# Gates of an mLSTM as one pass over half-sequence rows, with a new order of the first 560 steps

## The chip, the cores and the metric

The kernel runs on one core of one Trainium2 chip. The metric is the device time of one execution in microseconds (us). The engines are TensorE (PE; PEld are its weight loads), VectorE (DVE), ScalarE (ACT), GpSimd (POOL) and SyncE (SP), which here only issues DMAs. Each engine works off its own queue in order.

## The reference, cut

An mLSTM attention over 4 batches, 8 heads, 768 tokens and heads of 40 is followed by a feed-forward block (320 to 2048 to 320) and a mixture of 8 experts of which each token takes one. The part that matters here:

```python
for t in range(S):
    m_new = np.maximum(f_gate[:, :, t] + m, i_gate[:, :, t])
    f_stab = np.exp(f_gate[:, :, t] + m - m_new)
    i_stab = np.exp(i_gate[:, :, t] - m_new)
    m = m_new
    C = f_stab * C + i_stab * outer(v_t, k_t)
    n = f_stab * n + i_stab * k_t
    h = C @ q_t
    y[:, :, t] = sigmoid(o_gate) * h / max(|n @ q_t|, 1)
h = x @ w_in                                   # x: y laid out as 3072 tokens x 320
x = (max(h, 0) + alpha * min(h, 0)) @ w_out
# then, with e the argmax of x @ w_gate:
# out = softmax weight * sigmoid(x @ w_output_gate)[e] * (relu(x @ w1[e]) @ w2[e])
```

## The kernel before

**Tiling.** The attention runs in 24 units: 4 batches (b) times 6 chunks (c) of 128 tokens, all 8 heads at once. Three units make a block of 384 tokens, and the feed-forward block takes 8 such blocks times 16 slices of 128 hidden columns, 128 products `ph` (code F, line 916) and 128 accumulations `acc` (code S, lines 950 to 953). The expert weights stream through the core meanwhile (el, es, et: load, split in two float parts, store). After about 537 us comes the expert phase, which the change leaves alone. Weights of the feed-forward block arrive as 64-bit words: each of 16 slices of `w_in` (li) and `w_out` (lo) is loaded into one of three buffers `raw`, decoded by three DVE instructions (di, do; lines 655, 657, 659) and split in a high and a low part by ACT and by DVE or POOL (si, so). From each slice of `w_out`, PE also makes three transposes (gw, `pw`), ACT copies them (gc), and PE multiplies them with the routers' weights (gv, `pwg`, six instructions).

**A unit of attention.** `kt` are keys times a gate (pt), `pd` their products with the values (ad), `state` the running state (au: mask, then decay and add). `D` is a matrix of decays, loaded from the DRAM tensor `gd` with a broadcast (load_g) and raised to exponentials on ACT (ae, line 749). `ps` are scores (as), multiplied with D (am) and applied to the values, `pa` (ab). `pb` is the history (ah), normalised into `hN` (an) and added (aa); ay has the steps that divide and gate the result, and ac and ax transpose it into the feed-forward block's input.

**The gates before.** `gi` and `gf` hold 32 rows (batch and head), three times over, by 768 tokens. Three parts cover 1, 2 and 3 chunks. In each, one scan gives the running maximum `m` (line 549), differences follow, and scans by chunk give the cumulative sum `G` (line 566), stored in `gd`. `w` holds three sets of 32 rows: exp(G), exp of the key weights, and an exponent offset. PE transposes it by chunk (`pe_ek`, line 595) into `EKT`, which pt, an and ae read; `pe_dec` (line 613) spreads the decay of each chunk over 120 rows into `DEC`, which au reads. The parts are tied by the last maximum, `mlast`.

**What sets the order.** Every engine's order is the order in which the program names the work. For the first phase that is the list `ORDER`: codes of steps, each next use of a code being the next item of its kind. Sets in `OTHER` choose the second of two engines for single items of a kind. Buffers are few: three PSUM banks for attention, two for `ph`, three tiles `xr` and two `v`, which the gates share with the transposed weights and with the activations, and two `so`, which the gates' input shares with the output gates. A load waits in SP's queue, with all behind it, until its buffer is free.

Of the kernel before, what the change touches and what calls it, by code (L numbers as in the profile page):

```python
# [17 lines left out]
P = 128  # L18
# [6 lines left out]
E = 8  # L25
# [26 lines left out]
        0, 1, 3, 4, 5, 6, 7, 9, 15, 17, 20, 22,  # L52
    ),
    "prep_kt": (
        0, 1, 2, 3, 4, 7, 8, 9, 13, 14, 15, 16,
    ),
    "att_y": (
        3, 4, 6, 7, 11, 13, 16, 17, 18, 19, 20, 21, 22, 23,
    ),
    "expert_split": (  # L60
        0, 2, 3, 5, 6, 7, 8, 10, 12, 13, 14, 15, 18, 19, 20, 25, 26, 27, 30, 31, 32, 33, 34, 35, 36, 37,
        38, 39, 40, 41, 42, 43, 44, 45, 46, 47, 48, 49, 50, 51, 52, 53, 54, 55, 56, 57, 58, 59, 60, 61,
        62, 63,
    ),
    "gates_w": (
        0, 2,
    ),
    "split_wi": (
        1, 5, 6, 7, 8, 9, 11, 13, 14,
    ),  # L70
    "split_wo": (
        1, 3, 5, 6, 8, 9, 11, 13, 14, 15,
# [5 lines left out]
for _n, _w in (  # L78
    ("ident", P), ("stri", P), ("ones", P), ("bmask", 123),
    ("iota32", 32), ("iota128", P), ("tokv", U), ("rev", E), ("rst", E * (U - 3)),  # L80
    ("indb", B), ("nmin", E), ("nadd", E),
):
    CONST_COLS[_n] = (_o, _w)
    _o += _w
CW = _o

# [6 lines left out]
ah si li li so ad di di di ae lq lo aa gc ay si ay gv load_g load_gates ay di an sg lo di si ay au ah do gs di ae  # L93
lq an as do di load_g load_g lv do gw lo am gates di so do do ac ax lq lq si ab gc lo lo ae do ae aa ay ay ay as ay
gw lo am ab lv do do lg so ac gates_g gates_st gv do gates_w gc aa ay ay ay ay li gv log ac so ax do do gs gs li gw
gates_e do do do do gates_d load_g load_g gc ax lo so so gw gc gw gc pt lo F ad pt do do do gw load_g di di so F di
au f gv si di di di ad F do gs f el ah au g S ae do do si lg lg lg an do as gc ae am F f gw do load_g so g do li
load_g gv gv gs f di di li li ah S es F as gc et g S ab lo di lv gs ae so si di di gw ae an li di f F am g S aa di
g load_g gv ay ay di F li di si si log f pt do do F do gw gs lq di gv gc gv ay di di sg ay si di ac g gc gs ad F S
f di di so ab ax f g ae li di li si pt au aa ay ah ae an load_g lv ae g di di f F lo do do lo si lv di do S S di di  # L100
li li lq F S g gw ay ay lg gs gv lq load_g el f ay as so gc g F S S di am di ac di si f f pt do do do F g g load_g
S ax si ad di ab gs di sg aa ad lv au es au f S as so ae di si F am ab ae gw g S ay ay lo gv f ay li di aa di do ay
do gc gv et load_g ay gs ac ah ae di lg ay F g S el gs si load_g load_g as ax load_g f do F el el ay pt F an g S es
am ab es f f g et et so es gw ay ae gc ae g F f F gv gs ah S an aa g f g lq ay ay et el log ay ad au bo el el es es
F f F f lg load_g ae S ac ax load_g lv ae S pt et g S g es ah an lq lv ad au F f ay g F f S as am lq ah an F f et
ab aa ay S g g ac ax el ay et es lv el F f F f as am S g es load_g ae lg lg et ay lq ay S sg S et g F f ab aa ay
load_g bp lg S g ac ax S pt el ad au F f F f S g g S el el es lq es F f g F f g ay ay ay ah an pt S pt S et es F f
S et g F f log ad au g ae et as am ae S bo F f g F f load_g ae ab aa ay el lv el S g ay es el F f as am g load_g
load_g es et es et F f load_g ac ax lv ah an el el ae ae lg lg S g S S F f g ad au pt ah an ay es F f g ab aa F f
ay ad au et ae et S g el load_g el F f es ay et F f ay ay ac ax S g es ae S g ah an F f S S et es ay et g lv el el  # L110
bp as am F f F f el g es et pt S S ab aa ac ax g ad au F f F f g S g ay lq sg es es S ay lv pt F f ay el lq g F f
as am S g F f et es ah an ad au S log S g bo F f sg et g load_g load_g ay el el F f lg S ae ab aa ay ay ay et S F f
S g lq lq S g ae ac ax lg el S as am lv load_g load_g load_g es et es et ay F f pt F f g g ab aa ae ay ac ax F f S
g es ay ay ay S F f F f ae as am lq S g g load_g ah an ad au ac ax ae el F f lv pt el ae g et ab aa ay ay S es es F
f et et g load_g ay F f S g as am ay lv S load_g S F f g F f ah an ab aa ay S el el es ad au lg ay ae g ay el es F
f ac ax g load_g et et ah an ah an lv es et ae bp ay S S S ae as am F f g F f load_g bo g ab aa ae load_g ae F f g
S lq el S ac ax F f g load_g pt S pt F f lg load_g ae as am el es lq F f S g S el g es et F f et g ay ay el F f ae
ab aa g ay ay ay F f load_g lv F f S lq S ad au g g es et es et el ad au pt ae ac ax S F f g S el el as am F f F f
log g S S g es et lg bp es et F f F f g S g S load_g el S es et F f g F f log el el ae ay ay g S S bo es F f lg F f
ah an g S es as am sg ay et et g F f g lq ab aa ay S F f g el el S es load_g load_g sg F f F f S g ay ad au g es ae  # L120
ac ax et S lv et ay ay pt F f es F f ah an ab aa ay ay lg el ae g S g es ay lv ad au pt S F f F f el g ac ax ah an
et es et S load_g ay ae g el el F f es S g lg S ad au F f et es F f lq et et g el el ac ax bp S g S S F f g F f S
es es g F f g et S S bo as am el es F f F f g et lv pt el el et as am ab aa ay es et ay ay load_g S S g lg el
load_g first_set ah an lq ab aa el ay ay F f g F f S g ad au ae es F f F f lv es g S g ac ax S S ae ay ay ay as am
et et es et ac ax F f g F f S el el el bp g F f ah an ab aa g es es ay ay ay ay F f F f S S S g g et es et el S et
el F f g F f el S es es g F f et et ac ax g S S es et F f g ld el el F f g S F f g S bo ld es F f F f S g g route_a
S F f F f S g el g S bh bh bh et ld ld ld ad au bh ld ld bh bh bh F f ld S ld es S ld ld g es F f g bh bh S bh bh F
f g F f S et bh ld g ld S bp F f F f ld bh g bh bh bh bh S S bh route_first bh bh bh g F f route_first2 first_rows
S g F f g ld S F f F f S ld ld g S ld ld ld pt ld ld g first_x first_x S bo bp et first_1 route_b first_1 route_c
first_t first_s first_tl route_c2 first_t first_tl first_s first_2 first_2 route_d first_st first_2 first_2  # L130
"""


STEPS = {
# [72 lines left out]
def mlstm_moe_kernel(  # L207
# [264 lines left out]
    with ExitStack() as p1:  # L472
# [95 lines left out]
        def gates_st(part):  # L568
            c0, c1, o = GPARTS[part]
            nc.sync.dma_start(gd[:, c0 * P : c1 * P], gx[part][0][: B * H])  # L570
# [840 lines left out]
```

## Time and profile before

| | us |
|---|---|
| median of 3 timed runs | 776.0 (774.91 to 776.02) |
| profiled execution | 773.82 |
| its span, first to last instruction | 772.0 |
| PE busy in it | 749.9 |
| DVE, ACT, POOL busy | 472.8, 365.2, 181.4 |

The time around the span is 1.8 us. An instruction's duration is from one profiled execution. PE's instructions overlap in the records: a group's first start to the next group's first start is the pace. Float products of 32 bits are recorded as two instructions each.

### The profile page before, as it was taken

The numbers are of one execution on the slowest core, as the hardware profiler recorded it, in microseconds if no ns is written. First come the engines' busy times: TensorE is split into PE (matmuls) and PEld (weight loads), VectorE is DVE, ScalarE is ACT, GpSimd is POOL, SyncE is SP. The second block draws the span as 40 slices with busy tenths as digits, with TensorE's granted clock in tenths as the row PEclk, the third lists the DMA queues.
The fourth block names the chain that finished last, engine by engine and source line by source line (L and its number), as shares of the span: only waits on it lengthen the run. The fifth ranks groups of instructions, "written<-read, shape, count | busy, mean of one in ns | idle before, by whom it ended". The sixth has DMA issues, their size and how long they took to land.

```text
span 772.0 us, 15194 instructions
## 1 busy us (share of the span) xinstructions
PE 749.9 (97%) x4911; PEld 714.1 (92%) x4911; DVE 472.8 (61%) x1148; ACT 365.2 (47%) x812; POOL 181.4 (24%) x236
## 2 busy tenths in 40 slices
PE   4999999899999999999999999999999999999997
PEld 4889999899999999999999999998999999999996
DVE  6889997757865675777687786867332223223222
ACT  3646766654754555654565354434333333323322
POOL 2444523421231323100000000012222222223223
PEclk9999999999999999999999999999999999999999
DMA  7857869967687967757877968895977744931100
GB/s 227 274 176 199 275 186 292 299 229 242 205 307 253 286 239 222 252 179 273 294 255 267 298 227 292 288 332 201 373 320 269 277 166 170 418 134 36 42 13 22
DMA packets 81787, 179.64 MB, mean 233 GB/s; under 512 B 8700, under 2 KB 39481, under 8 KB 80428
## 3 DMA queue, kind: packets, MB, share of 16 engines
q1 hardware_dynamic: 78252, 169.92, 64.0%
q0 software_dynamic: 3456, 8.71, 3.3%
q8 instruction: 45, 0.74, 0.4%
q14 instruction: 34, 0.28, 0.1%
HBM read 246.55 MB, written 55.59 MB: 391 GB/s over the span
## 4 chain that ended last, share of the span: by engine, by line
PE 80%; DVE 10%; DMA 5%; ACT 3%; issue 2%; POOL 0%; SPq 0%; POOLq 0%; ACTq 0%; DVEq 0%
PE ph L916 19%; PE po L314 13%; PE p L314 13%; PE acc L950 6%; PE acc L951 6%; PE acc L953 6%; PE pa L846 4%; PE p L412 3%; PE ps L759 3%; DMA r_wi<-in_wi_dram 2%; PE pd L811 2%; DMA D<-gd 2%; PE pb L781 1%; PE xt L374 1%; DMA er<-in_ew_dram 1%
## 5 line engine op out<-in xcount | busy, mean ns | idle before, releaser
L916 PE MATMUL ph<-ring 128*128 128x384 f32 x1024 | 198.9, 342 | 0.3 <-DVE ring L938 0.3
L916 PEld LDWEIGHTS ph<-ring 128*128 128x128 f32 x1024 | 178.0, 189 | 2.8 <-DVE ring L938 1.0
L950 PE MATMUL acc<-ring 128*128 128x336 f32 x384 | 123.3, 326 | 0.6 <-ACT ring L937 0.3
L951 PE MATMUL acc<-ring 128*128 128x336 f32 x384 | 119.7, 317 | 0.2 <-DVE ring L716 0.2
L929 ACT ACTIVATE v<-ph 128x384 f32<-128x384 f32 x128 | 62.0, 488 | 103.7 <-PE ph L916 103.5
L434 DVE TENSOR_SCALAR yo<-po,xg 128x320 f32<-128x320 f32 x26 | 14.3, 551 | 137.4 <-PE po L314 137.4
L314 PE MATMUL po<-ring,hh 128*128 (+1 forms) x432 | 95.6, 308 | 0.0
L931 DVE SCALAR_TENSOR_TENSOR ph<-v,al,ph 128x384 f32<-128x384 f32 x104 | 63.9, 619 | 49.2 <-ACT v L929 48.9
L314 PE MATMUL p<-ring,xh 128*128 (+1 forms) x324 | 89.9, 399 | 0.0
L953 PE MATMUL acc<-ring 128*128 128x336 f32 x384 | 80.1, 316 | 0.0
L314 PEld LDWEIGHTS po<-ring,hh 128*128 128x128 f32 x432 | 73.2, 187 | 2.3 <-ACT hh L414 0.2
L938 DVE TENSOR_TENSOR ring<-ph,ring 128x384 fp32r<-128x384 f32 x104 | 57.4, 554 | 29.2 <-ACT ring L937 28.1
L950 PEld LDWEIGHTS acc<-ring 128*128 128x128 f32 x384 | 72.2, 188 | 2.3 <-ACT ring L937 1.0
L951 PEld LDWEIGHTS acc<-ring 128*128 128x128 f32 x384 | 72.2, 188 | 0.5 <-DVE ring L716 0.5
L937 ACT ACTIVATE ring<-ph 128x384 fp32r<-128x384 f32 x104 | 50.6, 488 | 43.6 <-DVE ph L931 36.6
L414 ACT ACTIVATE hh<-p 128x512 fp32r<-128x512 f32 x54 | 29.5, 596 | 86.4 <-PE p L412 86.4
L314 PEld LDWEIGHTS p<-ring,xh 128*128 128x128 f32 x324 | 58.8, 188 | 11.5 <-DMA ring<-scr 0.2
L314 PE MATMUL po<-ring,hl 128*128 (+1 forms) x216 | 66.6, 308 | 0.2 <-DVE hl L416 0.2
L435 POOL DMA_INDIRECT out_dram<-yo,tok x28 | 28.1, 1005 | 161.0 <-DVE yo L434 128.9
L401 ACT ACTIVATE hr<-p 128x512 f32<-128x512 f32 x56 | 33.6, 600 | 67.5 <-PE p L314 62.9
L953 PEld LDWEIGHTS acc<-ring 128*128 128x128 f32 x384 | 63.6, 189 | 0.0
L749 ACT ACTIVATE D<-D,EKT 128x128 f32<-128x128 f32 x192 | 60.7, 393 | 3.9 <-DMA D<-gd 3.7
(201 smaller groups left out, 1189.9 us busy)
## 6 DMA issues: line engine op xcount, KB each, us to landing
ring<-scr SPq DMA_DIRECT2D x26, 3072.0 KB
ring<-scr SPq DMA_DIRECT2D x26, 2560.0 KB
ring<-scr SPq DMA_DIRECT2D x33, 512.0 KB
D<-gd SPq DMA_DIRECT2D x48, 256.0 KB
er<-in_ew_dram SPq DMA_DIRECT2D x32, 384.0 KB
scr<-ring SPq DMA_DIRECT2D x32, 384.0 KB
scr<-er SPq DMA_DIRECT2D x32, 384.0 KB
er<-in_ew_dram SPq DMA_DIRECT2D x32, 320.0 KB
```

What stands on the lines that cost most here:

```text
L314: mm = T.matmul(o_, lhsT, r, start=start, stop=stop)
L401: A.activation(hr_half(j, hf), ph, AF.Relu)
L749: A.activation(d[:, j], d[:, j], AF.Exp, bias=EKT[:, c, i + j : i + j + 1])
L846: T.matmul(pa[:, h * 41 : (h + 1) * 41], t["D", h // 4][:, h % 4], v1[:, h * 41 : (h + 1) * 41], start=True, stop=True,)
L916: T.matmul(ph[:, :384], wi_[i][lo][:, wc], xTs[n % 2][:, xc], start=(a == 0), stop=(a == len(PASSES) - 1),)
L929: A.activation(v, ph[:, :384], AF.Relu, scale=-1.0)
L931: V.scalar_tensor_tensor(g, v, al1[:, i : i + 1], ph[:, :384], ALU.mult, ALU.add)
L937: A.activation(gh, v, AF.Copy)
L938: engine(V, G, "ffn_split", k).tensor_tensor(gl, v, gh.bitcast(F32), ALU.subtract)
L950: T.matmul(ac, gh[:, sl], hi, start=(i == 0), stop=False)
L951: T.matmul(ac, gh[:, sl], lo, start=False, stop=False)
L953: T.matmul(accs[n][t][:, :NO], gl[:, t * P : (t + 1) * P], hi, start=False, stop=(i == NFC - 1))
```

## The change

All six chunks' gates are worked out in one pass. A row is now a batch and head and a remainder k, and holds the chunks k and k + 3 in two groups of 128 columns; 96 rows hold everything once. Within a chunk two scans (a sum and a minimum) need nothing from other chunks. One product with `grep` (gates_b) brings the ends of all chunks to every row, where a scan of six columns gives the maximum at each chunk's start (gates_m). Then come the exponentials (gates_e), three transposes for each half (gates_t, `pe_ek`), and one set of products for all decays (gates_d). The constants are loaded in two pieces, the second late in the order; the selectors become wider and share the `so` buffers. The steps au and ay are cut in two, with the state update in a step av of its own. Single items of an, au and of the row normalisation (att_r) go from DVE to ACT, as 8 or 3 activations each, and the sets in `OTHER` change for the splits, `kt` and y. The list `ORDER` is new for about the first 560 steps; behind that it only has the additional codes av and ay.

```diff
-    "gates_w": (
-        0, 2,
+    "att_n": (
+        3, 5,
+    ),
+    "att_r": (
+        5,
+    ),
+    "att_u": (
+        2, 3, 6,
+    ),
+    "att_v": (
     ),
...
-    ("ident", P), ("stri", P), ("ones", P), ("bmask", 123),
+    ("ident", P), ("bmask", 123), ("stri", P), ("ones", P),
...
+CW0 = CONST_COLS["stri"][0]
...
-lo do lo do do do do load_gates load_cst gw so gc do lo gw gates gates_g load_gates gates_w gates_e load_wg lv do
-do do gw set_al1 gates gates_g gates_w gates_st gv li load_sel lo gc gc lv pt ad au so load_g so gates_st gs
-gates_d lq load_g load_g do gv gs gv gates_e di di gates_d do do pt li as ae gw gs ae di log lg lg ah an am di ab
...
+load_gates load_sel ga ah lo do do do lo do do do gb gm load_cst gw load_wg gc an gw gc so li so di ge gv gv gs gt
+lv lo gates_d do do do gw lq gs di pt so ad au gc gt gates_st lv as di li di load_g load_g pt load_g ae ae di di am
+gv av ab aa si li si lo lg gs di log ae do do do ay ay ay ay lg ad sg ay lq load_g load_g lo au lo lv di load_g lq
+gw di ah av an gc gv gs si ac ax as do do ae am do lo do do ah ab load_g do so so an li ae aa log ay ay ae ay ay lo
+lo gw gw gc gc lq as ay do do do am ac di di di so lo ax do ab aa so si do ay ay gw ay ay do do load_g ay gc gv gs
+set_al1 do load_g do gv gs gv gs pt so ac ax li di di so gw ae ae gc gw gc F F di si f li load_g f gv gs log do do
+do di di g so lg lg gv gs el es g lv ad au F F lq di f lq lo av S lo ae pt as am S lq ah si g do do do do do f ad
...
+        gcon = rp.tile([P, 471], F32, tag="so", name="gcon")[:GR]
+        sel, grep, gkm, gik = gcon[:, :360], gcon[:, 360:456], gcon[:, 456:459], gcon[:, 459:]
...
+        def load_gates():
+            nc.sync.dma_start(ti, gi)
+            nc.sync.dma_start(tf, gf)
+
+        def gates_a():
+            F, u = (hp.tile([P, 384], F32, tag="v", bufs=2, name=nm)[:GR, : 2 * P] for nm in ("gF", "gu"))
+            a, GG = (hp.tile([P, XW], F32, tag="xr", bufs=3, name=nm)[:GR, : 2 * P] for nm in ("ga", "gG"))
+            gx.update(F=F, u=u, a=a, GG=GG)
+            for js in halves:
+                V.tensor_tensor_scan(F[:, js], onesP, tf[:, js], 0.0, ALU.mult, ALU.add)
+            V.tensor_tensor(a, F, ti, ALU.subtract)
+            for js in halves:
+                V.tensor_tensor_scan(u[:, js], onesP, a[:, js], 1e30, ALU.mult, ALU.min)
+            km = gkm.unsqueeze(1).to_broadcast([GR, 2, 3])
+            for q, (x, o) in enumerate(((u, P - 1), (F, P - 1), (a, 0))):
+                xs = x.rearrange("p (j t) -> p j t", j=2)[:, :, o]
+                V.tensor_tensor(st[:, q], xs.unsqueeze(2).to_broadcast([GR, 2, 3]), km, ALU.mult)
+
+        def gates_b():
+            pg = ps_att("pe_g")
+            T.matmul(pg[:GR, :18], grep, small[:, :18], start=True, stop=True)
+            gx["pg"] = pg
+
+        def gates_m():
+            pg, u, a, GG = gx["pg"], gx["u"], gx["a"], gx["GG"]
+            V.tensor_copy(mf, pg[:GR, 6:13])
+            V.tensor_copy(mn[:, 0:1], mf[:, 6:7])
+            V.tensor_tensor_scan(mn[:, 1:6], pg[:GR, 0:5], mf[:, 0:5], 1e30, ALU.min, ALU.subtract)
+            mj = [x.rearrange("p (j k) -> p j k", j=2) for x in (mk, mn)]
+            V.tensor_tensor(mj[0], mj[1], gkm.unsqueeze(1).to_broadcast([GR, 2, 3]), ALU.mult)
+            V.tensor_reduce(ms, mj[0], AX.X, ALU.add)
+            for j, js in enumerate(halves):
+                V.tensor_scalar(GG[:, js], u[:, js], ms[:, j : j + 1], 0.0, ALU.subtract, ALU.min)
+            for j, js in enumerate(halves):
+                V.tensor_scalar(a[:, js], a[:, js], -1.0, ms[:, j : j + 1], ALU.mult, ALU.add)
+
+        def gates_st():
+            nc.sync.dma_start(gd, gx["GG"])
+
+        def gates_e():
+            F, u, a, GG = gx["F"], gx["u"], gx["a"], gx["GG"]
+            for j, js in enumerate(halves):
+                A.activation(u[:, js], a[:, js], AF.Exp, bias=GG[:, (j + 1) * P - 1 : (j + 1) * P])
+            A.activation(F, GG, AF.Exp)
+
+        def gates_t(j):
+            pe_ = ps_att(f"pe_ek{j}")
+            for y, x in enumerate((gx["F"], gx["u"], gx["a"])):
+                T.transpose(pe_[:, y * GR : (y + 1) * GR], x[:, halves[j]], ident[:GR, :GR])
...
+            pd = ps_att("pe_dec")
             for gq in range(3):
                 T.matmul(
-                    pd[:120, gq * B * nn : (gq + 1) * B * nn],
+                    pd[:120, gq * U : (gq + 1) * U],
...
+                if engine(V, A, "att_n", u) is A:
+                    for h in range(H):
+                        A.activation(hN[:, h], pbv[:, h], AF.Copy, scale=eg[:, h : h + 1])
+                else:
+                    V.tensor_tensor(hN, pbv, eg.unsqueeze(2).to_broadcast([P, H, 41]), ALU.mult)
...
+                if engine(V, A, "att_u", u) is A:
+                    for hh in range(3):
+                        cs = slice(hh * 41, (hh + 1) * 41)
+                        A.activation(v3(out)[:, :, cs], v3(dl)[:, :, cs], AF.Copy, scale=C("bmask", 120)[:, hh * 41 : hh * 41 + 1])
...
         def load_cst():
-            nc.sync.dma_start(cst, consts)
+            nc.sync.dma_start(cst[:, :CW0], consts[:, :CW0])
+
+        def load_cst2():
+            nc.sync.dma_start(cst[:, CW0:], consts[:, CW0:])
```

In the list, ga, gb, gm, ge and gt stand for gates_a, gates_b, gates_m, gates_e and gates_t. F first stands at place 198 of the old list and 192 of the new one.

## Rows read from the trace of the kernel before

**Rows 1.** The page: busy us, share of span, instructions.

```profile
PE 749.9 (97%) x4911; PEld 714.1 (92%) x4911; DVE 472.8 (61%) x1148; ACT 365.2 (47%) x812; POOL 181.4 (24%) x236
```

**Rows 2.** By stage: stretch, length, engines' busy us, clock, DMA share, GB/s.

```profile
0.00:7.01 7.01, 0.00 (x0) 0.03 (x1) 2.99 (x6) 1.75 (x2) 2.07 (x7) 1.00 0.71 230
7.01:23.09 16.08, 12.91 (x62) 11.55 (x63) 12.88 (x39) 7.95 (x25) 5.66 (x8) 1.00 0.85 246
23.09:56.78 33.69, 30.60 (x151) 27.61 (x150) 29.16 (x76) 16.83 (x41) 13.79 (x18) 1.00 0.69 213
56.78:165.00 108.22, 105.32 (x755) 101.42 (x754) 92.57 (x213) 67.55 (x166) 40.80 (x48) 1.00 0.78 242
165.00:540.00 375.00, 374.38 (x2569) 365.37 (x2568) 266.29 (x673) 199.73 (x447) 60.24 (x100) 1.00 0.76 260
540.00:772.00 232.00, 226.65 (x1383) 208.13 (x1381) 68.94 (x146) 71.37 (x134) 58.89 (x58) 1.00 0.48 186
```

**Rows 3.** PE in order of time: start us, us, work, idle before.

```profile
7.01 1.51 PE L696 MATMUL pw<-cst,f_wo 128*128 128x128 f32 x6 [7.01 <-DMA cst<-in_consts_dram]
...
23.09 3.48 PE L846 MATMUL pa<-kv,D 128*128 128x41 f32 x16
...
30.06 1.46 PE L709 MATMUL pwg<-wgt,woT 128*128 128x16 f32 x6 [0.85 <-DVE hN L796]
...
52.94 0.74 PE L595 MATMUL pe_ek<-cst,w 96*128 96x96 f32 x3 [0.31 <-ACT w L592]
...
54.31 1.34 PE L613 MATMUL pe_dec<-gin,sel 32*120 32x12 f32 x6 [0.63 <-ACT EKT L596]
...
56.78 2.91 PE L916 MATMUL ph<-ring 128*128 128x384 f32 x8
...
60.79 1.66 PE L916 MATMUL ph<-ring 128*128 128x384 f32 x8
...
62.28 0.73 PE L709 MATMUL pwg<-wgt,woT 128*128 128x16 f32 x6
```

**Rows 4.** Chain of waits, 0 to 60 us: start us, us, what.

```profile
0.83 3.03 DMA r_wo<-in_wo_dram
...
21.57 6.13 DMA r_wi<-in_wi_dram
...
46.45 1.05 DVE G L566 x3
```

**Rows 5.** DVE's groups by line, 0 to 60: count, busy us, mean ns.

```profile
L566 DVE TENSOR_TENSOR_SCAN G<-cst,g 96x128 f32<-96x128 f32 x6 | 2.2, 408 | 0.2
...
L555 DVE COPY mlast<-m 96x1 f32<-96x1 f32 x3 | 0.4, 142 | 0.0
...
L551 DVE MEMSET g<- 96x1 f32 x1 | 0.1, 59 | 0.0
```

**Rows 6.** Groups by line and shape, DVE, ACT, POOL, 0 to 120.

```profile
L554 DVE TENSOR_TENSOR g<-gin,m 96x127 f32<-96x127 f32 x1 | 0.3, 286 | 0.0
...
L796 DVE TENSOR_TENSOR hN<-pb,EKT 128x328 f32<-128x328 f32 x5 | 2.5, 495 | 0.4 <-PE pb L781 0.4
...
L749 ACT ACTIVATE D<-D,EKT 128x128 f32<-128x128 f32 x60 | 18.9, 391 | 0.1
...
L715 ACT ACTIVATE ring<-pwg 128x16 fp32r<-128x16 f32 x13 | 2.3, 179 | 8.9 <-PE pwg L709 8.9
...
L727 POOL TENSOR_TENSOR kt<-kv,EKT 128x320 f32<-128x320 f32 x5 | 4.1, 818 | 10.3 <-ACT EKT L596 4.3 <-issue 3.8 <-DMA kv<-in_kv_dram 2.2
```

**Rows 7.** Two DMAs of SP's queue, 0 to 30: start us, us.

```profile
8.69 0.33 SPq L570 DMA_DIRECT2D gd<-G  x1
...
10.99 0.38 SPq L741 DMA_DIRECT2D D<-gd  x1
```

**Rows 8.** Whom PE waited for, 56.78 to 165: us, times, longest.

```profile
PE pd L811 <- POOL kt L727: 1.6, 1, 1.6
...
PE acc L950 <- ACT ring L937: 0.3, 1, 0.3
```

More of the change, by code (lines that the diff above doesn't have):

```diff
@@ L94 @@
[L94 to L103, printed above, removed]
@@ L139 @@
     "load_cst": ("load_cst", [()]),
-    "load_gates": ("load_gates", zip(range(3))),
+    "load_cst2": ("load_cst2", [()]),
+    "load_gates": ("load_gates", [()]),
     "li": ("load_wi", zip(range(16))),
@@ L145 @@
     "lq": ("load_q", zip(range(24))),
-    "gates": ("gates", zip(range(3))),
+    "ga": ("gates_a", [()]),
+    "gb": ("gates_b", [()]),
+    "gm": ("gates_m", [()]),
     "lv": ("load_kv", zip(range(24))),
@@ L154 @@
     "au": ("att_u", zip(range(24))),
+    "av": ("att_v", zip(range(24))),
     "aa": ("att_a", zip(range(24))),
@@ L172 @@
     "ab": ("att_b", zip(range(24))),
-    "ay": ("att_y", [(i, j) for i in range(24) for j in range(4)]),
+    "ay": ("att_y", [(i, j) for i in range(24) for j in range(5)]),
     "set_al1": ("set_al1", [()]),
@@ new lines, in mlstm_moe_kernel @@
+        onesP, small = gin[:GR, 0, 2 * P :], gin[:GR, 1, 2 * P :]
+        G.memset(onesP, 1.0)
+        st = small[:, :18].rearrange("p (q j k) -> p q j k", q=3, j=2)
+        mn, mk, ms = small[:, 18:24], small[:, 24:30], small[:, 30:32]
+        dec = small[:, 32:56].rearrange("p (b j k) -> p b j k", b=B, j=2)
+        mf = small[:, 56:63]
+        halves = [slice(j * P, (j + 1) * P) for j in range(2)]
+        def load_gates():
+            nc.sync.dma_start(ti, gi)
+            nc.sync.dma_start(tf, gf)
@@ L609, in gates_d @@
                 ALU.mult,
             )
-            pd = ps_att(f"pe_dec{part}")
+            pd = ps_att("pe_dec")
             for gq in range(3):
                 T.matmul(
-                    pd[:120, gq * B * nn : (gq + 1) * B * nn],
+                    pd[:120, gq * U : (gq + 1) * U],
                     sel[:, gq * 120 : (gq + 1) * 120],
-                    dec.rearrange("p b c -> p (b c)"),
+                    small[:, 32:56],
                     start=True,
@@ L619, in gates_d @@
                 )
-            for gq in range(3):
-                V.tensor_copy(
-                    DEC[:, gq].rearrange("p (b c) -> p b c", b=B)[:, :, c0:c1],
-                    pd[:120, gq * B * nn : (gq + 1) * B * nn].rearrange("p (b c) -> p b c", b=B),
-                )
+            A.activation(DEC.rearrange("p g u -> p (g u)"), pd[:120, : 3 * U], AF.Copy)
         stp = p1.enter_context(tc.tile_pool(name="stp", bufs=2))
         hp = p1.enter_context(tc.tile_pool(name="hp", bufs=3))
-        mlast = wp.tile([GR, 1], F32, name="mlast")
-        onesP = C("ones")
         raws = {}
@@ L878, in att_y @@
                 yv = y[:, :DM].rearrange("p (h d) -> p h d", h=H)
-                V.tensor_tensor(yv, pa[:, :, :D], t["dn"].unsqueeze(2).to_broadcast([P, H, D]), ALU.mult)
+                if engine(V, A, "att_r", u) is A:
+                    for h in range(H):
+                        A.activation(yv[:, h], pa[:, h, :D], AF.Copy, scale=t["dn"][:, h : h + 1])
+                else:
+                    V.tensor_tensor(yv, pa[:, :, :D], t["dn"].unsqueeze(2).to_broadcast([P, H, D]), ALU.mult)
+            elif step == 4:
+                y = t["y"]
                 eng = engine(G, V, "att_y", u)
```

222 lines of the change are left out of this document (86 added, 136 removed).

## The prediction

> **What bounds the kernel now.** I read the page's shares first, then busy time by stage, then TensorE (PE) in order of time, then the chain of waits for the first stretch. The page [rows 1] says that PE is busy 97% of the span and no other engine over 61%: what can be won is PE's idle time and whatever makes its instructions slow. The table by stage [rows 2] says where the idle time lies. I cut it where PE starts (7.01 us), at the first half of the first unit's weighted values (`pa`, 23.09), at the first product of the feed-forward block (`ph`, 56.78), at 165 and at 540. Idle time is the stretch less PE's busy time: 7.01, 3.17, 3.09, 2.90, 0.62 and 5.35 us. The last two lie where the change does nothing, so 16.2 us are in its reach, 13.3 of them ahead of the first `ph`.
>
> Slow instructions are the second part. The granted clock reads 1.00 in every stretch [rows 2], yet the first `ph`, eight products of 128x384 at 56.78, took 2.91 us and the next one, at 60.79, took 1.66; six products into `pwg` took 1.46 at 30.06 and 0.73 at 62.28 [rows 3]. That is the ratio of the two levels, 1.2 and 2.4 GHz: PE worked at the lower one until some 3 us after the first `ph` began, whatever the clock column says. So a PE instruction ahead of the first `ph` costs twice what it costs behind it, and the 30.60 us that PE is busy from 23.09 to 56.78 are at half rate.
>
> In that stretch PE is the nearest thing to a bound (30.60 of 33.69), but VectorE (DVE) stands beside it with 29.16 [rows 2], and the chain of waits runs through DVE almost alone: the gate scans `G` are links of it, and ahead of them a load of first-layer weights that landed 6.13 us after issue [rows 4]. From 56.78 on, PE is dense and only order matters: PE has to do all its work in turn, so the end moves by what moves ahead of it.
>
> **Gates, part by part.** Before, a row is a batch and head and the gates come in three parts of 1, 2 and 3 chunks, each a chain of scans. After, a row is a batch, a head and every third chunk, so two column groups of 128 hold all six, and one small product carries the running maximum across. DVE loses thirteen groups of gate instructions, 10.9 us in all ([rows 5] has the largest, one of the middle and the smallest of the thirteen). It gains four scans of 0.41 (1.6), one 256-column difference (0.4), four 128-column operations at 0.28 (1.1, the 127-column difference [rows 6]), and some nine tiny ones at 0.14 as `mlast` [rows 5] (1.3): 4.5 us. **DVE: 6.4 us less**, all ahead of the first `ph`.
>
> PE loses six transposes and twelve decay products and gets six transposes, six decay products and the small product. What counts is the third part's share: 0.74 of `pe_ek` and 1.34 of `pe_dec` at 52.94 and 54.31, and the waits of 0.31 and 0.63 ahead of them [rows 3]. These 3.0 us sit shortly before the first `ph` and go. The second part's share is done earlier instead, as the new gt and gates_d; the small product is bounded by one `pe_dec` group, 0 to 0.5 us, and lies where PE waits anyway.
>
> **The front chain.** Everything up to the first weighted values now hangs on one chain, and I walked it with rows. Loads: a weight load issued at 0.83 took 3.03 us [rows 4], so the gates, half as large, land at about 3.5. Then 2.5 us of DVE come at once (four scans, the difference, three tiny ones), and the decoding of the first two weights follows instead of leading, so the first transposes of weights start at 7.0 to 7.8 (now 7.01, on the constants [rows 3], of which only a third is now loaded first; at the 230 GB/s of [rows 2] the load shrinks by 1.4 us). The joining (five tiny ones and the four of 128 columns, 1.8 us of DVE) ends near 10.4. The exponentials wait on ScalarE (ACT) behind the second copy of transposed weights, which shares three buffers with two gate tiles and so waits for the first `pwg`: they end near 12.8; transposes 0.7 [rows 3], copy 0.4 and scaled keys 0.8 [rows 6], behind PE's decay products and the next weight's transposes: `pd` starts near 15.5 and the scores near 17.5. The store of the gates goes at 10.4 instead of 8.69, its load returns 2.3 us after the store's issue as now [rows 7], and ACT reaches the decay matrices only behind the second gate copy, near 18. `pa` comes near 21.4 instead of 23.09, but with one weight's transposes and one `pwg` group (0.7 and 1.5) undone that are done by then today: **level**. Bounds: 1.5 us either way, the width of the 7.0 to 7.8 start and of one queue position on ACT.
>
> **The order.** Ahead of the first `ph` the new order has the same nine transposed weights, three units of attention and two updates of the state, and one `pwg` group more (7 for 6): 1.46 us at half rate there, 0.73 less behind it [rows 3], so 0.7 lost. Of the 3.09 us of PE's waits after 23.09, 0.94 are counted above; the other 2.15 end on DVE or on what DVE decodes. DVE loses about a sixth of its work there, so I take half of them as gone, **1.0 us** (0 to 2.15).
>
> Behind the first `ph`, 2.90 us of waits are left in the reach, 1.6 of them one wait for scaled keys (`kt`) on GpSimd (POOL) [rows 8]. DVE had 92.57 of 108.22 us there [rows 2]; it now carries less, but ACT and POOL carry more. I take a quarter as gone, **0.7 us** (2.9 gained to 2 lost). The moved steps also carry their loads past SP's queue: part of the constants (316 KB) goes behind, the gate loads shrink from 576 to 192 KB, and the selectors grow from 45 to 181 KB. The first expert piece is split soon after its load is issued; I find some 5 us of other PE work covering it. These I cost at nothing; the cover is PE's queue of `ph` and `acc`.
>
> **Onto ACT.** Two normalisations of history, one of rows and three maskings move from DVE to ACT: 24 and 9 small activations. DVE saves some 0.5 for each of the six [rows 6], 3 us. ACT pays between 0.18 (128x16, no bias) and 0.39 (128x128, with bias) each [rows 6]: 5.9 to 12.9 us. I take the low end, as the width of 41 is nearer to 16. ACT was busy 67.55 of 108.22 us, so it is hidden unless a block stands in front of a copy that PE waits for. The Trainium skill, "ScalarE: Activation LUTs", Rules for kernel authors, speaks against this: it budgets about 0.3 us and 0.83 ns per element for each activation with a pointer operand. The row with a bias (0.39 for 128 columns) agrees; by it a block of eight would be an estimated 2.7 us instead of 1.4, near the high end.
>
> **Sum.** 3.0 + 1.0 - 0.7 + 0.7 = 4.0 us less. The profiled execution took 773.82 (span 772.0, 1.8 around it) and would take 769.8; the median of the timed runs is 776.0, 2.2 above it, and I carry the difference over: **772.0**. Its own range, with the front chain's 1.5 and the later waits, is 769.5 to 774.5.
>
> **Rivals.**
> 1. More comes free (15%): the front chain gains its 1.5, all of the 2.15 goes, and half of the later 2.90: 3.0 + 1.5 + 2.15 - 0.7 + 1.5 = 7.4 less, 768.6. For it: DVE leads the chain. Against: PE itself is 91% busy in that stretch.
> 2. Nothing to speak of (19%): PE at half rate is the true bound. The 3.0 of the third part stays, but the front chain loses its 1.5, waits only change places, and the extra group costs 0.7: 0.8 less, 775.2. For it: 30.60 of 33.69. Against: the third part's work is really gone.
> 3. Slower (18%): ACT becomes the bound of the stretch to 165. Its place: blocks of 1.4 to 3.1 us in front of the copies that feed `acc`, in units 2, 3, 5 and 6. Its price: if every block is paid in full, 5.9 at the low end, against the 4.0: 777.9. It decides from where the lead of `ph` over `acc` is used up. For it: one of PE's later waits already ends on an ACT copy [rows 8]. Against: 38% of ACT's time there is free.
>
> **Chances.** My forecast has 48%, the rivals 15, 19 and 18. A measurement of this kernel can tell about 0.2% (1.6 us) from no change. Faster takes rival 1 and nearly all of the forecast: 61%. Rival 2 and the edge of the forecast are the same: 21%. Rival 3 is slower: 18%. The range reaches from below rival 1's middle to beyond rival 2, 767.5 to 776.8, and leaves out rival 3 and some of rival 1.
>
> **What would show it.** Right: the first `ph` near 54.3 with seven `pwg` groups ahead of it; `pe_ek` and `pe_dec` only before 20; DVE some 6 us less busy up to there; the first `pa` at 20 to 23; the half-rate times again end some 3 us after the first `ph`; idle time from there to 165 near 2.2. Wrong: a first `pa` past 25 (front chain), waits for `ring` from ACT (rival 3), a first `ph` at 56 or later (rival 2), or a clock that rises at another place, each microsecond of which moves the end by half of one.

## The result: 9.3 us faster, more than forecast

The changed kernel took 764.98 us (median of 6 runs, 761.90 to 766.29), the kernel before 774.25 beside it (6 runs). The ratio is 0.9873, 95% interval 0.9847 to 0.9899. The direction was as forecast, the size more than twice the 4.0 us, and the time lies below the range, which ended at 767.5. The 772.0 also started from a median of 776.0 (three runs of the kernel before), and beside the changed kernel that one took 774.25: of the 7.0 us that the forecast is off, 1.75 come from there and 5.3 from the gain. The profiled execution took 763.64, its span 761.8 (before 773.82 and 772.0).

The page of the changed kernel, against [rows 1]: PE has 5.9 us less to do, DVE 8.1 less, ACT 1.9 more.

```profile
PE 744.0 (98%) x4907; PEld 711.0 (93%) x4907; DVE 464.7 (61%) x1119; ACT 367.1 (48%) x840; POOL 182.6 (24%) x240
```

Its table by stage, against [rows 2] (stretch, length, busy us of PE, PEld, DVE, ACT, POOL, granted clock, DMA share, GB/s), cut at PE's start, the first `pa`, the first `ph`, 165 and 540:

```profile
0.00:6.42 6.42, 0.00 (x0) 0.00 (x1) 2.26 (x9) 1.28 (x1) 1.31 (x7) 1.00 0.63 188
6.42:20.96 14.54, 11.71 (x64) 10.51 (x64) 10.86 (x31) 7.56 (x24) 3.69 (x5) 1.00 0.82 265
20.96:50.88 29.92, 29.53 (x149) 27.21 (x150) 26.41 (x66) 16.23 (x42) 11.79 (x17) 0.52 0.77 236
50.88:165.00 114.12, 112.00 (x816) 109.20 (x815) 94.60 (x207) 77.07 (x203) 49.49 (x59) 0.99 0.77 248
...
540.00:761.80 221.80, 216.12 (x1317) 198.37 (x1315) 65.28 (x133) 68.06 (x128) 55.16 (x54) 0.99 0.47 180
```

Length less PE's busy time gives the idle time: 6.42, 2.83, 0.39 and 2.12 us up to 165. Before it was 7.01, 3.17, 3.09 and 2.90. The third stretch is the news: between the first `pa` and the first `ph` PE now waits for next to nothing.

PE in order of time, against [rows 3] (start, us, engine, line, work, count, idle before and its releaser):

```profile
6.42 0.51 PE L577 MATMUL pe_g<-gin,gcon 96*96 96x18 f32 x2 [6.42 <-DVE gin L573]
7.71 0.90 PE L699 MATMUL pw<-cst,f_wo 128*128 128x128 f32 x3 [0.78 <-DVE f_wo L662]
...
13.78 1.29 PE L622 MATMUL pe_dec<-gin,gcon 96*120 96x24 f32 x6
...
17.50 1.81 PE L762 MATMUL ps<-q 40*128 40x128 f32 x16
19.25 0.84 PE L712 MATMUL pwg<-wgt,woT 128*128 128x16 f32 x6
20.96 2.65 PE L858 MATMUL pa<-kv,D 128*128 128x41 f32 x16 [0.87 <-DVE D L770]
...
44.92 3.86 PE L712 MATMUL pwg<-wgt,woT 128*128 128x16 f32 x18
...
50.88 3.91 PE L934 MATMUL ph<-ring 128*128 128x384 f32 x16
```

The first `ph` stands at 50.88, where the forecast had 54.3 and the kernel before 56.78. No `pe_ek` or `pe_dec` stands behind 20 us.

The chain of waits of the first stretch, against [rows 4], runs from the gates' load over their scans to ACT's decay matrices:

```profile
1.29 2.67 DMA gin<-in_gf_dram
...
4.40 0.41 DVE gF L566
...
17.92 2.44 ACT D L752 x8
```

I need one more marker: the first product of the routing (`within`), up to which all the attention and feed-forward work lies. It starts at 488.74 before and at 478.24 after: 10.5 us are won ahead of it and 0.3 lost behind it, which makes the span's 10.2. This row of the kernel before covers its work from the first `ph` to there (columns as above):

```profile
56.78:488.74 431.96, 428.73 (x2979) 417.99 (x2978) 320.40 (x753) 247.37 (x569) 94.08 (x133) 1.00 0.77 254
```

### The profile page after: what moved, and what is told of

The parts are those of the page before. It is cut to its first block, busy times and chain, and to the rows that moved or that the text cites. A ratio compares the mean times of both kernels' runs of the same rounds, so it can differ in the third digit from the quotient of the medians.

```text
span 761.8 us, 15188 instructions
## 1 busy us (share of the span) xinstructions
PE 744.0 (98%) x4907; PEld 711.0 (93%) x4907; DVE 464.7 (61%) x1119; ACT 367.1 (48%) x840; POOL 182.6 (24%) x240
## 4 chain that ended last, share of the span: by engine, by line
PE 85%; DVE 7%; DMA 2%; ACT 2%; issue 2%; POOL 1%; SPq 0%; POOLq 0%; ACTq 0%; DVEq 0%
PE ph L934 22%; PE po L326 13%; PE p L326 13%; PE acc L968 7%; PE acc L969 7%; PE acc L971 7%; PE pa L858 4%; PE p L424 3%; PE ps L762 3%; PE pb L784 1%; PE pd L815 1%; PE xt L386 1%; PE pt L911 1%; ACT D L752 1%; DMA er<-in_ew_dram 1%
## 5 line engine op out<-in xcount | busy, mean ns | idle before, releaser
L326 PEld LDWEIGHTS p<-ring,xh 128*128 128x128 f32 x324 | 58.8, 188 | 11.5 <-DMA ring<-scr 0.2
```

The lines of the kernel that those rows point to most:

```text
L326: mm = T.matmul(o_, lhsT, r, start=start, stop=stop)
```

## The experiments

Each kernel is the changed one with the edit shown, unless it says otherwise. Times are medians, beside runs of the kernel before on the same chip (773.8 to 774.7).

### The changed kernel once more (x0)

> The changed kernel once more, unaltered, as the mark for the others of this call and for PE's clock. If the clock's early rise near 19 us in its first profile belongs to the kernel, this profile shows it again, PE is busy some 2.2 us less ahead of the first ph than its work at half rate takes, and the time is 9 to 10 us below before. If it was chance, the first ph comes up to 2 us later (near 53) and the time is 7 to 8 below before.

763.96 us, ratio 0.9873 (0.9835 to 0.9912). In the first profile the `pwg` group at 19.25 took 0.84 us, full rate, ahead of a granted clock that then read 0.52 on average from 20.96 to 50.88. In this one there was no such rise:

```profile
19.23 1.46 PE L712 MATMUL pwg<-wgt,woT 128*128 128x16 f32 x6
20.52 3.62 PE L858 MATMUL pa<-kv,D 128*128 128x41 f32 x16
...
50.83 4.34 PE L934 MATMUL ph<-ring 128*128 128x384 f32 x16
```

The first `ph` came at the same place, 50.83. So the early rise is chance, and it bought nothing: without it, the expectation had that product up to 2 us later and a time 7 to 8 us below before, and it is 9.8. By stage:

```profile
20.52:50.83 30.31, 30.12 (x150) 28.21 (x151) 26.13 (x66) 16.26 (x42) 11.51 (x17) 1.00 0.78 232
50.83:476.81 425.98, 425.26 (x2974) 416.77 (x2973) 316.89 (x738) 251.01 (x598) 100.98 (x141) 1.00 0.78 258
```

This quiet execution is the one that I set others against.

### The new gates in the old order (x1)

The order and the engines of the kernel before; only the steps of the gates are exchanged:

```diff
-load_gates load_cst ... gates gates_g ... gates_w gates_e
+load_gates load_sel load_cst load_cst2 ... ga gb gm ... gates_st ge gt gt gates_d
```

> The new gates alone: the old order with the new gate steps at the place of the first part's, the old choice of engines, nothing moved to ACT. Theory gates (the gain is the gate work itself, less of it on DVE and no third part ahead of the first ph): most of the gain is here, 5 to 7 us below before, first ph near 52 to 53. Theory order (the gates only made room; the gain comes from steps moved): at most 2 us below before, PE's waits ahead of the first ph only change their place, first ph at 55 or later.

774.46 us, ratio 1.0001 (0.9982 to 1.0019): in the old order the gates are worth nothing, as the expectation's theory of the order had it.

```profile
0.00:25.88 25.88, 13.71 (x66) 12.32 (x67) 13.55 (x41) 9.51 (x27) 5.84 (x14) 1.00 0.71 213
25.88:56.45 30.57, 28.46 (x142) 25.95 (x141) 24.77 (x63) 15.77 (x39) 11.06 (x15) 1.00 0.72 212
```

From the first `pa` to the first `ph` it saves 3.1 us (30.57 for 33.69), as the sum had it. But all gates now stand ahead of the first `pa`, and in the old order that comes at 25.88 instead of 23.09, 2.8 later: PE waits 6.9 us for the constants and 2.6 for the gates' exponentials. In the second stretch DVE is no busier than in x0 (24.77 of 30.57 us, there 26.13 of 30.31), and still PE waits 2.1 us, nearly all of it for DVE.

### Nothing moved onto ACT (x2)

```diff
-    "att_n": (3, 5,),
-    "att_r": (5,),
-    "att_u": (2, 3, 6,),
+    "att_n": (),
+    "att_r": (),
+    "att_u": (),
```

> The changed kernel with the 33 small activations put back as six DVE instructions. If DVE's relief by these counts, DVE's 3 us come back as waits behind the first ph: 1 to 3 us above the changed kernel. If ACT's load costs more than it frees (my third rival): 1 to 4 us below it. If neither engine is late there: within 1 us of it.

763.01 us, ratio 0.9855 (0.9816 to 0.9893); first `ph` at 51.29. The 33 small activations neither cost nor gain anything that can be measured. What they take on ACT in the changed kernel (to 165 us, by line and shape: count, busy us, mean ns, idle before):

```profile
L803 ACT ACTIVATE hN<-pb,EKT 128x41 f32<-128x41 f32 x16 | 3.2, 310 | 1.6 <-PE pb L784 1.6
L833 ACT ACTIVATE pd<-pd,cst 120x123 f32<-120x123 f32 x6 | 2.0, 342 | 0.1
...
L893 ACT ACTIVATE y<-pa,dn 128x40 f32<-128x40 f32 x8 | 1.6, 310 | 0.3 <-DVE dn L887 0.3
...
L833 ACT ACTIVATE state<-pd,cst 120x123 f32<-120x123 f32 x3 | 0.9, 364 | 0.9 <-PE pd L815 0.9
```

### DVE loaded again (x3)

```diff
+        def dve_more(i):
+            V.tensor_tensor(spare, spare, spare, ALU.add)
```

Twelve of these stand evenly between the first scaled keys and the first `ph`. The expectation had 6.6 us for them; in the trace they take 7.4 (618 ns each).

> The changed kernel with 12 additions of 128x384 on DVE (some 6.6 us) spread between the first scaled keys and the first ph: the gate work given back to DVE and to no other engine. Theory DVE (the waits that went were DVE's): PE waits 2.5 to 4 us more ahead of the first ph, which comes near 53.5 to 55, and the time is 2.5 to 4 us above the changed kernel. Theory PE (half-rate work was the bound, DVE had room): less than 1 us above it.

768.72 us, ratio 0.9933 (0.9910 to 0.9956), 4.8 above x0.

```profile
20.97:54.83 33.86, 30.91 (x150) 28.18 (x150) 31.41 (x75) 15.81 (x41) 11.71 (x15) 1.00 0.69 204
```

Against x0's row, DVE has 31.41 for 26.13, PE's idle time goes from 0.19 to 2.95, and the first `ph` from 50.83 to 54.83. PE's busy time grows by 0.8. So in the new order the waits of that stretch hang on DVE's load, though DVE had 4.5 us free in it before [rows 2].

### Idle products to raise the clock (x4, x5)

x4 puts eight products of 128x512 at the very start; x5 has one more behind every step of PE ahead of the first feed-forward step. Their results are not used.

```diff
-load_gates load_sel ga ah lo do do do lo do do do gb gm
+load_gates load_sel ga ah lo do do do lo do do do warm warm warm warm warm warm warm warm gb gm
```

> The changed kernel with eight idle 128x512 products on TensorE at the very start, while it waits for the gates; their results are not used. My theory: the granted clock is not what sets the first feed-forward product, because VectorE is 90% busy there; in one of the two profiles of the changed kernel an early rise (a pwg group at 0.84 instead of 1.46) left that product where it was (50.88 and 50.83). So the first weighted values come up to 1 us earlier (19.5 to 20.5), the clock falls again, the first feed-forward product stays at 50.0 to 51.0 and the time within 1 us of 764.0. Rival: instructions at half rate set the front. Then an earlier rise that lasts lets the 42 us of TensorE work ahead of that product shrink, it comes at 46 to 48, and the time is 759 to 761.

> As x4_warm_front, and one more idle 128x512 product behind every step of TensorE ahead of the first feed-forward step. It asks what the half rate costs up to there. If these hold the clock up (a pwg group of six in 0.73 instead of 1.46), TensorE's work ahead of the first feed-forward product halves from 42 to 21 us, and VectorE, with 39.4 us of work up to there behind loads of 2.3 us, becomes the only bound: that product at 45 to 48, time 759 to 762. If they do not hold it up, each costs 0.43 at half rate in TensorE's queue and the product comes 5 to 13 us later, time 769 to 777. My theory, in which VectorE bounds the front already, gives no more than 3 us of gain even if the clock stays up.

x4: 764.67 us, ratio 0.9892 (0.9859 to 0.9925). The clock rose (a `pwg` group in 0.96), fell at 9.3, rose once more at 26, fell again at 33:

```profile
8.76 0.96 PE L711 MATMUL pwg<-wgt,woT 128*128 128x16 f32 x6
10.36 1.46 PE L711 MATMUL pwg<-wgt,woT 128*128 128x16 f32 x6 [0.65 <-ACT woT L704]
...
27.20 0.84 PE L711 MATMUL pwg<-wgt,woT 128*128 128x16 f32 x6 [0.35 <-ACT woT L704]
...
50.00 4.70 PE L933 MATMUL ph<-ring 128*128 128x384 f32 x16
```

From its first `pa` (20.30) to there, PE was busy 27.60 us, 2.5 less than in x0, and the stretch became 0.6 shorter: the rest turned into waits, 1.5 us of them for DVE. In x5's profiled execution, its slowest of five (770.26), the products did not hold the clock up either: single ones took 0.77 us, then 0.48, then 0.77 again, and the first `ph` came at 58.94:

```profile
31.58 0.48 PE L1281 MATMUL warm<-ring 128*128 128x512 f32 x1
...
39.27 0.77 PE L1281 MATMUL warm<-ring 128*128 128x512 f32 x1
...
58.94 2.96 PE L934 MATMUL ph<-ring 128*128 128x384 f32 x16
```

The other four executions of x5 took 761.5 to 765.6, the median is 764.59 (ratio 0.9853, 0.9826 to 0.9880). Their mean clock is higher on record (0.988 to 0.993, the profiled one 0.982), but no trace shows where, nor their first `ph`; so what the clock does to the front in x5 stays open. None of the five beats the changed kernel by more than the runs of that one differ.

### Where the gain behind the first `ph` comes from (x6, x11)

x6 moves seven attention steps behind the next feed-forward step, so that PE changes between plain products and the rounded ones (`ph`, `acc`) 14 times more. x11 moves eleven lone steps to their neighbours, 22 changes less.

```diff
 x6:  -F F S as S   +F F S S as        (the pattern, seven times)
 x11: -as S ah ad gw   +as ah ad gw S  (the pattern, eleven times)
```

> The changed kernel with seven attention steps of TensorE behind the first feed-forward step moved one feed-forward step later, so that plain and rounded products alternate more often: 14 more changes of kind, the same instructions. Theory of grouping: each change of kind costs 0.06 to 0.12 us, so TensorE's work between the first feed-forward product and the routing product grows by 0.8 to 1.7 us at waits no larger than 1 us, and the time goes from 764.0 to 765 to 766. Rival: what the changed kernel gains behind the first feed-forward product is only waits; then this time stays within 0.3 us of 764.0, or grows by waits that the trace shows.

> The changed kernel with eleven steps of TensorE behind the first feed-forward products, each of which stood alone between steps of the other kind, moved behind the next group: 22 fewer changes between plain and rounded products, the same instructions. It is the opposite of x6_split. By the price that x6_split gave (0.8 us of TensorE's work for 14 changes, 0.06 each, beside some 2 us of new waits), TensorE's work from the first feed-forward product to the routing product falls by 1.0 to 1.6 us below 425.3. If no wait arises from the later steps, the time is 762 to 763; if they cost as much as in x6_split, 764 to 766. If the work does not fall, the price of a change of kind is not real.

x6: 766.87 us, ratio 0.9894 (0.9867 to 0.9922). x11: 777.84, ratio 1.0050 (1.0023 to 1.0076), 14 us slower than what it was made from. The waits of x6 in this stretch grew from x0's 0.7 us to 4.1, where its expectation had at most 1. From the first `ph` to `within`, x6 and then x11:

```profile
50.36:482.98 432.62, 428.53 (x2973) 418.58 (x2972) 315.76 (x738) 250.93 (x598) 102.92 (x141) 0.99 0.77 254
```

```profile
51.10:492.14 441.04, 432.07 (x2974) 422.40 (x2973) 317.55 (x738) 250.92 (x598) 100.30 (x141) 0.99 0.76 249
```

The expectation for x11 failed. Its waits in the stretch are 9.0 us for x0's 0.7, the longest of them one of 2.90 us at 65.36 for decoded words on ACT. And the clock fell twice; the second time (columns as in the table by stage):

```profile
116.00:120.00 4.00, 3.77 (x36) 3.54 (x34) 3.93 (x6) 4.00 (x14) 2.79 (x5) 1.00 0.70 203
120.00:130.00 10.00, 9.19 (x42) 8.78 (x42) 4.47 (x11) 3.35 (x10) 1.55 (x2) 0.66 0.97 292
```

Length times what the clock lacks, halves of it: 10 us at 0.66 cost 3.4, and 86 to 92 at 0.72 another 1.7. That is 5.1 of the 6.8 us that PE was busy longer than in x0; the 1.7 left have the wrong sign for the theory, which had PE's work fall. x6 had one fall (84 to 90 at 0.72, 1.7) and a later rise after the first `ph` (4.90 for 4.34, 0.6); of its 3.3 us more, 1.0 is left, which may or may not belong to the 14 changes. A price of one change seems to stand in the rows, and doesn't. In x11, the first `acc` behind a plain product is followed after 0.23 us, the next ones after 0.16 and less. But the three transposes ahead of it take 0.25 us up to its start, and three transposes ahead of plain products 0.33:

```profile
66.84 0.49 PE L698 MATMUL pw<-cst,f_wo 128*128 128x128 f32 x3
67.09 0.40 PE L967 MATMUL acc<-ring 128*128 128x336 f32 x1
67.32 0.32 PE L968 MATMUL acc<-ring 128*128 128x336 f32 x1
67.48 0.32 PE L967 MATMUL acc<-ring 128*128 128x336 f32 x1
...
82.73 0.49 PE L698 MATMUL pw<-cst,f_wo 128*128 128x128 f32 x3
83.06 1.41 PE L711 MATMUL pwg<-wgt,woT 128*128 128x16 f32 x12
```

The 0.08 us that the entry seems to cost are missing in the group ahead. It is the same in x0 (medians): `pd`, `pb` and `pt` take 0.56, 0.59 and 0.25 us up to a rounded product and 0.64, 0.66 and 0.34 up to a plain one. Only behind `pa` and `ps`, which are as long ahead of either, could part of the 0.08 be a price. So no price of a change is shown. The new order has 143 changes in this stretch, the old one 155; that is no measured part of the gain.

### The constants loaded whole (x7)

```diff
-load_cst gw load_wg gc
+load_cst load_cst2 gw load_wg gc
```

> The changed kernel with the second part of the constants loaded right behind the first, as one load would. In the kernel before, TensorE waited 7.01 us for the constants; in the changed one it starts at 5.7 to 6.4 on the gates. Theory that the cut of the constants is part of why the first weighted values come 2.1 to 2.6 us earlier: TensorE starts later or waits up to 1.4 us for weights or constants behind that load, the first weighted values come at 21.0 to 22.4 instead of 20.5 to 21.0, and the time is 764 to 766. Rival: the gates' own chain sets the front, and the later load was hidden; then all stays within 0.3 us, and the time at 764.

765.83 us, ratio 0.9899 (0.9857 to 0.9942), with a first `pa` at 20.72 and a first `ph` at 50.24. The first `pa` lies between those of the two profiles of the changed kernel (20.52 and 20.96): the rival was right, and the cut of the constants is hidden there. The median is 1.9 us above x0's, as the theory had it, but the four runs (762.61 to 767.78) lie across those of the changed kernel, so the time doesn't decide.

### Old gates in the new order, and half the new order (x8, x9, x10)

x8 is the kernel before with the new order; its gate steps stand where the new ones do, the third part's ahead of its use. x9 is x8 with the old steps in the old order up to the first `pa`. x10 is the changed kernel up to the first `pa`, and from there the old order. (In x8 and x9 the first unit of two blocks is multiplied by the output gate before its sigmoid is taken, so what they return differs; the instructions are the same.)

```diff
 x8, behind the front:
-load_gates ga gb gm ge gt gt gates_st gates_d
+load_gates load_gates gates gates_g gates_st gates_w gates_e ... load_gates gates ... gates_e gates_d
 x10, behind the first pa:
-si li si lo lg gs di log ae do do do ay
+set_al1 lo do do do gw gs log lg lg ah si li li so ad di ae
```

> The new order with the old gates: three parts of 1, 2 and 3 chunks, their steps put where the new gates stand or, for the third part, ahead of its first use, and the normalisations and masks all on VectorE. Theory that order and gates work only together: the third part's TensorE work (2.08 us in the old trace) is back ahead of the first feed-forward product and VectorE has its 6.4 us of gates and 3 us of normalisation again; the added 6.6 us of VectorE work cost 4.8 us in another run, so that product comes at 55 to 58 and the time is 769 to 773. Rival, the order alone carries it: that product at 51 to 53 and the time at most 767. The gain behind that product (grouping, one pwg group less) stays in both, some 4 to 6 us against the kernel before.

> Old gates in three parts, and the steps of the kernel before in their old order up to the first weighted values; from there on the new order, with the third part's gate steps put ahead of their first use, and normalisations and masks all on VectorE. It is the new order without the new gates, with a front that is known: the first weighted values at 23.1. Theory that gates and order work only together: VectorE has its old work back, the first feed-forward product comes at 55.5 to 58, the waits behind it are 2 to 5 us; but TensorE's work behind it up to the routing product is that of the changed kernel, 425 to 426 us and not 428.7, since it comes from the order alone. Time 769 to 774. Rival, the order carries it: that product at 52 to 54 and the time at most 768.

> New gates and the new order up to the first weighted values; from there on the steps in the old order. The first weighted values at 20.5 to 21.0. Theory: what comes ahead of the first feed-forward product is won by the gates with the new front: 2.1 to 2.6 us of front, 2 us of the third part's work, and its waits, so that product comes at 51 to 53, two to four microseconds early; behind it the old order keeps its 428 to 429 us of TensorE work and 3 to 4.5 us of waits. Time 767 to 771. Rival: the rest of the old order hands the front's gain back as waits, that product comes at 55 to 56.5 and the time is 772 to 775, as with the new gates in the whole old order (774.46).

x8: 787.99 us, ratio 1.0169 (1.0143 to 1.0194). x9: 779.37, ratio 1.0063 (1.0040 to 1.0087). x10: 783.25, ratio 1.0109 (1.0068 to 1.0150). All three are slower than either kernel, and slower than any theory had them. In x8 the gates' two chains stand one behind the other at the front: PE waits 8.5 us for the constants, 7.9 for the gates' exponentials and 5.4 for a decoded weight, and the first `pa` comes at 33.98. In x9 it comes at 22.85, but the first `ph` only at 62.16, with one wait of 5.1 us ahead of `pb` to which the profile gives no releaser. So neither measures what a well-fitted order without the new gates would take, and that stays open. One expectation held: PE's work behind the first `ph` is the new order's even with the old gates, as x9 shows.

```profile
62.16:491.63 429.47, 425.31 (x2973) 416.01 (x2972) 319.46 (x744) 244.30 (x565) 102.67 (x141) 1.00 0.77 255
```

x10 has the front (first `pa` at 20.61, first `ph` at 53.18) and loses it behind:

```profile
53.18:498.04 444.86, 436.18 (x2980) 424.61 (x2978) 321.57 (x740) 255.07 (x602) 101.11 (x141) 0.98 0.75 247
```

It waits 8.7 us there, and the clock falls three times, each time shortly behind waits. One of them, first the clock and then PE in order of time:

```profile
86.00:90.00 4.00, 2.98 (x22) 2.50 (x21) 2.57 (x7) 3.19 (x8) 1.70 (x3) 1.00 0.90 289
90.00:96.00 6.00, 4.84 (x22) 4.84 (x23) 5.48 (x14) 4.80 (x12) 2.79 (x4) 0.72 0.54 172
```

```profile
91.16 1.16 PE L814 MATMUL pd<-kv,kt 128*120 128x123 f32 x6 [1.97 <-DVE ring L718]
91.98 2.91 PE L933 MATMUL ph<-ring 128*128 128x384 f32 x8
...
98.61 1.66 PE L933 MATMUL ph<-ring 128*128 128x384 f32 x8
```

The three falls (70 to 76 and 90 to 96 at 0.72, 108 to 116 at 0.57) cost 1.7, 1.7 and 3.4 us.

## Why the prediction fell short

Its sum, cut at the markers, against what was measured:

| stretch | forecast | after | x0 |
|---|---|---|---|
| to the first `pa` | 0 | -2.1 | -2.6 |
| first `pa` to first `ph` | -2.5 | -3.8 | -3.4 |
| first `ph` to `within` | -1.4 | -4.6 | -6.0 |
| from there to the end | 0 | +0.3 | +0.4 |
| span | -4.0 | -10.2 | -11.5 |

The prediction fell short in all three stretches of the change: by 3.2 to 4.6 us behind the first `ph`, by 2.1 to 2.6 at the front, by 0.8 to 1.2 between. (The forecast's second row is 3.0 + 1.0 less 1.46 for the seventh `pwg` group, its third that group's 0.73 behind and the 0.7 of later waits.)

**The front chain: the walk was right, the bookkeeping wrong.** Forecast against the trace: `pd` 15.5 and 15.66, scores 17.5 and 17.50, first `pa` 21.4 and 20.96. The step that failed is "but with one weight's transposes and one `pwg` group undone that are done by then today: level". Three `pwg` groups stand ahead of the first `pa` in both kernels. I also charged the seventh group in the stretch behind, so one group was paid twice. With only the transposes undone (0.7), the walk itself gave a gain of 1.0, and 2.1 and 2.6 were measured.

**Waits up to the first `ph`: "I take half of them as gone".** Of 3.09 us, 0.39 are left in the first profile and 0.19 in x0; nearly all of the 2.15 went, not half. PE's busy time there fell by 0.5 in x0, against the 0.6 of the sum (2.08 less, 1.46 more). The step that failed is the half itself: the sum treated DVE's relief as a share of its work and left the order out. x3 shows that the relief is needed: with 7.4 us put back on DVE in the new order, 2.8 us of waits return. x1 shows that it isn't enough: in the old order, with the old choice of engines, DVE is as free, and of the 3.09 us only 1.0 went, about what the third part's own waits were (0.94). So it took both; which of the moved steps did it, no run shows. Rival 1, which had just this, had 15% and 768.6. It was the nearest, and still too small.

**Third part of the gates: 3.0, true but not by itself.** The stretch lost 3.1 us in x1 as well, yet x1 as a whole gained nothing, since all gates then stand ahead of the first `pa`. The new order is what keeps that chain short: x10 has it only up to there, and its first `pa` comes at 20.61. The cut of the constants has no part in it that x7 could show.

**Behind the first `ph`: the largest miss, a term left out.** The sum had 0.73 for the `pwg` group, and a quarter of the waits. Waits to `within` are 2.2 for 3.2 us in the first profile and 0.7 in x0. But PE's busy time fell by 3.5 us in x0, and I had priced 0.73 of it. The step that failed is to let the new order change nothing in PE's own work but that one group. Some 1.0 of the 3.5 is the scatter of a single execution: from the 257th product `ph` on, PE has the same steps in the same order in these kernels (the kernel before, x0 and x1, up to `within`):

```profile
192.85:488.74 295.89, 295.56 (x2037) 289.11 (x2036) 209.84 (x497) 164.91 (x375) 45.99 (x77) 1.00 0.76 257
```

```profile
182.26:476.81 294.55, 294.55 (x2038) 288.84 (x2037) 209.99 (x498) 164.82 (x375) 47.66 (x80) 1.00 0.78 261
```

```profile
194.47:488.92 294.45, 294.45 (x2037) 288.82 (x2036) 209.31 (x497) 164.70 (x375) 45.87 (x77) 1.00 0.78 258
```

Ahead of that product PE was busy 133.2 and 133.4 us in the old order (the kernel before and x1), and 130.7, 130.3 and 130.3 in the new one (x0, the first profile and x9): some 2.5 us go with the new order, with old gates or new. The `pwg` group is 0.73 of it. The clock is a second part: it rose 2.9 to 4.0 us after the first `ph` before [rows 3], and some 2.6 in x0 (its 16 products took 4.34 us, at full rate 3.04), and half of the difference is 0.2 to 0.7. Some 1.1 to 1.6 us stay unassigned. x11 shows that grouping alone doesn't bring them.

**Rival 2 (PE at half rate is the true bound) is out as forecast:** the waits went and did not change places. But what is left is close to it. PE is 99% busy from the first `pa` to the first `ph` in x0, and with 2.5 us less to do there x4 won 0.6: PE's work at half rate and DVE's feed bound that stretch almost alike.

**Rival 3 (ACT) is out.** The low end of 0.18 us for each small activation was too low: lines 803, 833 and 893 take 0.31 to 0.36, and 33 of them keep ACT busy for 7.7 us, not 5.9. The Trainium skill, "ScalarE: Activation LUTs", Rules for kernel authors, budgets about 0.3 us and 0.83 ns per element with a pointer operand, an estimated 0.33 us for 41 columns; the rows agree with 0.31. Still x2 shows that this is hidden. What the rival lacked is a copy that PE would wait for: in x0 none of PE's waits from the first `ph` to `within` is for ACT.

**What held:** seven `pwg` groups ahead of the first `ph`, no gate work behind 20 us, DVE 5.5 us less busy up to there (39.5 for 45.0), the rise of the clock some 3 us after the first `ph` (about 1.7 in the first profile and 2.6 in x0), idle time to 165 of 2.12.

## What to carry to other kernels

Where one engine feeds another step by step and both are over 85% busy, the feeder's relief is worth what the order of the steps makes of it: with 5.5 us less on DVE up to the first `ph`, the new order lost nearly all of its waits, and the old order kept 2.1 us of them with DVE as free. An algorithmic saving and the order have to be judged together: the gates without the order gave 0.0 us, and the gates with the new order only up to the first `pa` lost 8.6. Before a gain in busy time is explained, compare a stretch in which the order is the same: here 1.0 of 3.5 us was the scatter of one execution. A hand-written order is worth keeping whole: eleven local moves that looked harmless cost 14 us.

## What the runs showed of the hardware

Once PE works at full rate behind the first `ph`, the granted clock can still fall to 0.5 for 3 to 7 us, and a fall costs 1.6 to 1.7 us or 3.4 (length times what the clock lacks). The profiles of x2, x4, x5, x6, x7 and x8 have one such fall each, x11 has two and x10 three; the kernel before, both profiles of the changed one, x1, x3 and x9 have none. In x10 and x11 the falls come behind waits of 0.8 to 2.0 us. But a wait of 2.90 in x11 was followed by none, and in x5 and x7 PE was busy for all but 0.2 us of the four ahead of the fall. So waits alone don't decide it, and what does stays open. It is enough to hide an effect of 1 us in a single profile: compare the clock before the times.

The clock column reads 1.00 up to the first change that is recorded: at 30.06 in the kernel before, and at 19.23 in x0, `pwg` took 1.46 us under a column of 1.00. Up to the first `ph` the column shows less than 1.00 only in executions in which the clock rose and fell again. Durations of equal instructions tell the level where the column doesn't.

A group of PE's instructions can start earlier in the records than its pace tells: in x11, three transposes take 0.25 us up to the start of an `acc` and 0.33 up to that of a plain product, and that `acc` is followed 0.08 us later than one behind its own kind. A price that is read at one side of such a change is no price until the other side is added.
